# A fourth staging buffer, zeros moved to the K steps, and the weight-gradient stores of three groups moved to Pool's queue, in a decode-attention and FFN backward kernel

## The chip, the cores and the metric

One core of one Trainium2 chip. The metric is device time in microseconds (us), the median of several executions of the same program. A profiled execution gives a trace; its span, from the first to the last instruction, is some 1.8 us shorter than the time of that execution. The kernel before ran at 285.98 us (285.46 to 286.58, three executions). The core moves data with 16 DMA engines. Instructions on SP (SyncE), ACT (ScalarE) and Pool (GpSimd) put transfers into three queues, which the profile names q1, q10 and q0. Below, "the rings" are what waits in these queues, and a "hole" is a stretch in which they run dry and the rate falls.

## The reference

The kernel computes the output and all weight and input gradients of a layer that adds attention over a cache and a GEGLU FFN. Attention reads only the last 1024 of 4096 cache rows, but the gradients of the two caches are written whole, so three quarters of each are zeros.

```python
def _fwd_reference(A_x, A_k_cache, A_v_cache, A_wq, A_wo, B_x, B_w_gate, B_w_up, B_w_down):
    # attention: B=4, 32 heads of q, 8 of k and v, Dh=128, Sk=4096, window W=1024
    #   k, v = cache[:, :, Sk-W:, :];  o = softmax(q k^T / sqrt(Dh)) v;  o @ wo
    # ffn: (gelu(x @ w_gate) * (x @ w_up)) @ w_down      D=512, F=1792
    xn = _layernorm(x, axis=-1)
    return x + _A_ref(xn, ...) + _B_ref(xn, ...)

# outputs: (out, d x, d k_cache, d v_cache, d wq, d wo, d w_gate, d w_up, d w_down), bf16
# ... cut
```

The two cache gradients are 33.5 MB each. Of these, 64 rows of 786 KB (one for each batch and head of each cache) are zeros, 50.3 MB. That makes 81 MB written and 31 MB read.

## The kernel before

Heads are worked on in four groups, t = 0 to 3, of two K/V heads. For each group, scores run over V and K in eight steps each, softmax and its gradient follow, and each of dv and dk is evacuated from PSUM through staging buffers of 1 MB. `zeros(n)` queues n zero rows on ACT's queue. `bg` is a list of small pieces of work that `tick` puts between the matmuls.

```python
with tc.tile_pool(name="stage", bufs=3, reuse_waits="tile") as stage, ...:
    for t in range(NT):
        ...
        scores(t, 0, {})
        zeros(2 if t == 0 else 0)
        scores(t, 1, softmax(t))            # zeros(4) after each 2nd step of a head
        d1, d2 = softmax_d(t)
        zeros(4 if t >= NT - 2 else 0)
        ...
        odq(t); fin(t)
        load_next(t)                        # weights and K/V of group t + 2, Pool's queue
        tick(len(bg))
        dw(t)                               # pieces of dwo, dwq

# one dv or dk block of a head, 8 pieces
if jj == 0:
    held["stg"] = stage.tile([P, NQ, JQ, Dh], BF16, name="stg_" + nm, tag="stg")
... matmul into kv_ps, evac(stg[:, :, jj, :], mps[:], 512) ...
if jj == JQ - 1:
    store(nc.sync, out=og[:, t * GP + g, K0:Sk, :]..., in_=stg[:]..., ...)

# dw(t): four 0.52 MB stores a group, from the pool of four osb buffers
held["osb"] = outp.tile([P, rep, D], BF16, name="osb_o", tag="o")
...
store(nc.sync, out=out_5[...], in_=held["osb"][:], ...)

def zeros(n):
    zs = ztile[0:P:P // ZP, :]              # ZP = 64 partitions, 12 KB each
    ...
    z = store(nc.scalar, zdst, zsrc, "zeros", ["rest", "zeros"])
# ... cut
```

Of the kernel before, what the change touches and what calls it, by code (L numbers as in the profile page):

```python
# [13 lines left out]
BF16 = mybir.dt.bfloat16  # L14
P = 128
# [3 lines left out]
def kernel(  # L19
# [27 lines left out]
    nc = tc.nc  # L47

    B, Sq, D = A_x.shape
# [3 lines left out]
    rep = Hq // G  # L53
# [3 lines left out]
    ND = D // P  # L57
# [3 lines left out]
    GP = 2  # L61
    NT = G // GP
    HG = GP * rep
# [5 lines left out]
    CW = HG * Dh  # L69
# [177 lines left out]
                                  in_=tps[:].rearrange("p c (b r) -> p c b r", b=B)[:, :, :, 0:8])  # L247


    xnm = const.tile([P, rep, D], BF16, name="xnm")  # L250
    dym = ffn.tile([P, rep, D], BF16, name="dym")
    for src, dst in ((dy_b, dym), (xn_b, xnm)):
        for i in range(rep):
            nc.gpsimd.tensor_scalar(out=dst[:, i, :], in0=src[:], scalar1=msk_i[:, i:i + 1], scalar2=None,
                                    op0=ALU.mult)


# [124 lines left out]
    def masks(t):  # L382
        for k, nm in enumerate(("do", "q")):
# [3 lines left out]
                                        in1=msk[:, :, g].unsqueeze(2).broadcast_to([P, NQ, Dh]), op=ALU.mult)  # L387
            st[t][nm] = mr

    def scores(t, k, hooks):  # L390

        lf = (qm, dom)[k]
        blks = (k_t, v_t)[k]
        ps = ps_a.tile([P, WQ], FP32, name="S_ps", tag=("S", "dP")[k])
        for g in range(GP):
            for q in range(NQ):
                T_ps = ps_w.tile([P, JQ, P], BF16, name="T_ps", tag="w")
                for jj in range(JQ):
                    nc.tensor.transpose(T_ps[:, jj, :], blks[(t, g)][:, q * JQ + jj, :], ident[:])  # L399
                T_sb = tsb.tile([P, WQ, B], BF16, name="T_sb", tag="T", bufs=4)  # L400
                evac(T_sb[:].rearrange("p n b -> p (n b)"), T_ps[:].rearrange("p j m -> p (j m)"), 1024, half=True)
                s = q * GP + g
                for b in range(B):
                    nc.tensor.matmul(ps[b * RG:(b + 1) * RG, :], lhsT=lf[:, b, s * RG:(s + 1) * RG],  # L404
                                     rhs=T_sb[:, :, b], start=(g == 0 and q == 0),
                                     stop=(g == GP - 1 and q == NQ - 1), tile_position=(0, b * RG))
                for f in hooks.get(g * NQ + q, ()):
                    f()
                tick(2 if k or q % 2 else 1)
                if q == 1:  # L410
                    zeros(4 if (g, k) != (0, 0) else 0)
        st[t][("S", "dP")[k]] = ps[:]

    def by_batch(src, nm, eng):
# [133 lines left out]
    def dw(t):  # L548

        X = st[t]["X"]  # L550

        def piece_o(g, i, held):
            if i == 0:
                held["osb"] = outp.tile([P, rep, D], BF16, name="osb_o", tag="o")
            mps = ps_w.tile([P, D], FP32, name="dwo_ps", tag="w")
            nc.tensor.matmul(mps[:], lhsT=X[:].rearrange("p h d -> p (h d)")[:, g * rep + i:CW:HG], rhs=dyz[:], start=True, stop=True)  # L556
            evac(held["osb"][:, i, :], mps[:], 512)
            if i == rep - 1:
                store(nc.sync, out=out_5[t * CW:(t + 1) * CW, :].rearrange("(p k) n -> p k n", k=HG)[
                    :, g * rep:(g + 1) * rep, :], in_=held["osb"][:], kind="rest", apart=["zeros", "rest"])  # L560

        def piece_q(c2, k, held):
            if k == 0:
                held["osb"] = outp.tile([P, 2, GP, rep * Dh], BF16, name="osb_q", tag="o")
            ci, g = k // GP, k % GP
# [3 lines left out]
                             rhs=X[:, g * rep:(g + 1) * rep, :].rearrange("p i d -> p (i d)"), start=True, stop=True)  # L569
            evac(held["osb"][:, ci, g, :], mps[:], 512)  # L570
            if k == 2 * GP - 1:
                store(nc.sync,
                      out=out_4.rearrange("(p c) j -> p c j", c=ND)[:, c2 * 2:(c2 + 1) * 2, t * CW:(t + 1) * CW],
                      in_=held["osb"][:].rearrange("p c g j -> p c (g j)"), kind="rest", apart=["zeros", "rest"])

# [108 lines left out]

    acc_sum(0, [(lambda c, fc=fc: wd_sb[:, fc, c * P:(c + 1) * P], aT_b[:, fc, :]) for fc in range(NF)])

    def f_rows(srcT, nm):

        ps = od_ps[:]
        for f4 in range(NF4):  # L690
            for b in range(B):
                nc.tensor.matmul(ps[b * RB:b * RB + 4, f4, :], lhsT=srcT[:, 4 * f4:4 * f4 + 4, b], rhs=ident[:],
                                 start=True, stop=True, tile_position=(0, b * RB))
        rows = const.tile([P, NF4, P], BF16, name=nm)
        evac(rows[:], ps, 512)
        return rows

    a_r = f_rows(aT_b, "a_r")
    def piece_d(f4, i, n, held):
        if i == 0:  # L700
            held["osb"] = outp.tile([P, 4, D], BF16, name="osb_d", tag="o")
# [8 lines left out]
    def piece_g(s_r, og, c, i, held):  # L710
        if i == 0:
            held["osb"] = outp.tile([P, NF4, 4, P], BF16, name="osb_g", tag="o")
        n = (NF - i + 3) // 4
        mps = ps_w.tile([P, NF4, P], FP32, name="dwg_ps", tag="w")
        nc.tensor.matmul(mps[:, 0:n, :].rearrange("p f d -> p (f d)"), lhsT=xnm[:, i, c:D:ND],  # L715
                         rhs=s_r[:, 0:n, :].rearrange("p f d -> p (f d)"), start=True, stop=True)
        evac(held["osb"][:, 0:n, i, :], mps[:, 0:n, :], n * P)
        if i == 3:
# [9 lines left out]
    df_ps = ps_a.tile([P, ND, B], FP32, name="df_ps", tag="S")  # L728
    edge = dict(lhsT=ztile[0:1, 0:P], rhs=ztile[0:1, 0:ND * B])
    nc.tensor.matmul(df_ps[:].rearrange("p c b -> p (c b)"), start=True, stop=False, **edge)  # L730
    for srcT, wsb, og, nm in ((dhgT_b, wg_sb, out_6, "dhg_r"), (dhuT_b, wu_sb, out_7, "dhu_r")):
        s_r = f_rows(srcT, nm)
        for c in range(ND):
            held = {}
            for i in range(4):
# [17 lines left out]
    acc_add(1, df_ps[:])  # L753

    ffn_pools.close()
    with tc.tile_pool(name="stage", bufs=3, reuse_waits="tile") as stage, \
            tc.tile_pool(name="wodd", bufs=1, reuse_waits="tile") as wodd:
        wpool.append(wodd)
        kvpool.append(wodd)
# [3 lines left out]
        for t in range(NT):  # L763
# [4 lines left out]
            zeros(2 if t == 0 else 0)  # L768
            scores(t, 1, softmax(t))
            d1, d2 = softmax_d(t)  # L770
            zeros(4 if t >= NT - 2 else 0)
            if t + 1 < NT:
                pre(t + 1, {0: [d1], 2: [d2]})
            else:
# [78 lines left out]
```

## Time and profile before

| | before |
|---|---|
| time, median (range) | 285.98 us (285.46 to 286.58) |
| span of the profiled execution | 281.7 us (that execution took 283.50 us) |
| TensorE, VectorE, ScalarE, Pool busy | 75%, 56%, 41%, 20% |
| moved | 112.15 MB, mean 398 GB/s |
| plateau of the rate | 420 to 424 GB/s |

The page cuts the span into 40 slices. Its GB/s row says what the 16 DMA engines moved in each. The busy-by-stretch view gives the same for any stretch: length, busy time of PE (TensorE), PEld (weight loads), DVE, ACT and Pool, each with its number of instructions, then granted clock, DMA share and GB/s. The prediction shows the lines of both.

### The profile page before, as it was taken

To read this page: it belongs to the slowest core of one execution; us is meant where nothing else is said; L and a number is where in the kernel's file an instruction comes from. 1 tells how busy PE (TensorE), PEld (TensorE's weight loads), DVE (VectorE), ACT (ScalarE), POOL (GpSimd) and SP (SyncE) were. 2 spreads that over 40 slices of the span, in tenths; PEclk is the share of its full clock that TensorE was granted. 3 is DMA by queue.
4 is the path that set the end of the run, shared out by engine and by line. 5 is a ranking of instruction groups with operands and counts; after the bars stand their busy time and mean duration, and the time that the engine had idled before them with its cause. 6 is when DMAs were issued, how large, how long until landed. Compare 5 with 4: busy or idle time off the path is not lost.

```text
span 281.7 us, 7190 instructions
## 1 busy us (share of the span) xinstructions
PE 210.1 (75%) x3132; PEld 135.9 (48%) x3132; DVE 158.7 (56%) x336; ACT 115.6 (41%) x214; POOL 56.0 (20%) x56
## 2 busy tenths in 40 slices
PE   1968976968769699967793399786963996878950
PEld 0856854634536465534461265454641654526520
DVE  6945754626467457645672137547651465367691
ACT  1421743344535146535421335435502563571540
POOL 3890003400200633020024060110050201002000
PEclk9975999979988989999999559979995999799795
DMA  7999999999999999999999969999999779999995
GB/s 236 445 398 426 423 405 413 408 418 419 422 427 426 420 425 417 425 422 425 428 420 409 406 202 347 425 426 426 416 427 429 318 301 409 428 427 423 419 416 221
DMA packets 19407, 112.15 MB, mean 398 GB/s; under 512 B 1440, under 2 KB 5040, under 8 KB 10416
## 3 DMA queue, kind: packets, MB, share of 16 engines
q10 hardware_dynamic: 4384, 50.34, 42.4%
q1 hardware_dynamic: 12304, 44.58, 39.1%
q0 software_dynamic: 2688, 16.78, 15.1%
q8 instruction: 24, 0.39, 0.5%
q14 instruction: 7, 0.06, 0.0%
HBM read 30.68 MB, written 81.01 MB: 396 GB/s over the span
## 4 chain that ended last, share of the span: by engine, by line
PE 45%; DMA 27%; DVE 16%; ACT 4%; issue 3%; POOL 2%; ACTq 0%; DVEq 0%; SPq 0%
DMA out_dram<-stg_dv 18%; PE T_ps L399 10%; PE kv_ps L537 8%; PE S_ps L404 6%; DMA out_dram<-osb_d 6%; DVE T_sb L101 4%; DMA out_dram<-ztile 4%; PE dwo_ps L556 3%; PE acc_ps L213 3%; PE dwq_ps L568 2%; POOL P_x L417 2%; PE wqT_ps L595 2%; PE wgT_ps L742 2%; PE od_ps L509 1%; PE dwg_ps L715 1%
## 5 line engine op out<-in xcount | busy, mean ns | idle before, releaser
L101 DVE COPY T_sb<-T_ps 128x1024 bf16<-128x1024 bf16 x64 | 43.8, 691 | 41.2 <-PE T_ps L399 40.8
L99 ACT CAST stg_dk<-kv_ps 128x512 bf16<-128x512 f32 x40 | 22.2, 589 | 54.0 <-PE kv_ps L537 36.0
L99 ACT CAST stg_dv<-kv_ps 128x512 bf16<-128x512 f32 x57 | 30.4, 593 | 30.0 <-PE kv_ps L537 30.0
L537 PE MATMUL kv_ps<-qmr,dS_x 128*128 128x512 bf16 x64 | 22.9, 448 | 16.9 <-ACT stg_dk L99 15.3
L537 PE MATMUL kv_ps<-domr,P_x 128*128 128x512 bf16 x64 | 22.8, 427 | 5.4 <-POOL P_x L417 4.8
L101 DVE CAST stg_dk<-kv_ps 128x512 bf16<-128x512 f32 x24 | 16.1, 686 | 17.8 <-PE kv_ps L537 17.6
L399 PEld LDWEIGHTS <-kb 128*128 128x128 bf16 x256 | 18.6, 105 | 10.7 <-issue 7.8
L399 PE MATMUL T_ps<-ident,kb 128*128 128x128 bf16 x256 | 23.4, 231 | 0.0
L386 POOL TENSOR_TENSOR domr<-r,msk 128x512 bf16<-128x512 bf16 x8 | 8.2, 1040 | 71.2 <-DVE r L379 71.2
L99 ACT CAST osb_g<-dwg_ps 128x512 bf16<-128x512 f32 (+1 forms) x28 | 14.1, 540 | 18.4 <-PE dwg_ps L715 11.5
L399 PE MATMUL T_ps<-ident,vb 128*128 128x128 bf16 x256 | 21.3, 226 | 0.0
L399 PEld LDWEIGHTS <-vb 128*128 128x128 bf16 x256 | 16.6, 102 | 6.9 <-issue 5.0
L417 POOL TENSOR_TENSOR P_x<-P_b,bmsk 128x1024 bf16<-128x1024 bf16 x4 | 7.6, 1894 | 56.3 <-ACT P_b L465 56.3
L404 PE MATMUL S_ps<-T_sb,dom 128*32 128x256 bf16 x128 | 12.7, 387 | 8.0 <-DVE T_sb L101 7.5
L99 ACT CAST osb_o<-dwo_ps 128x512 bf16<-128x512 f32 x25 | 14.5, 587 | 9.3 <-PE dwo_ps L556 8.5
L99 ACT CAST osb_q<-dwq_ps 128x512 bf16<-128x512 f32 x25 | 14.3, 588 | 8.4 <-PE dwq_ps L568 7.8
L595 PEld LDWEIGHTS <-wq_sb 128*128 128x128 bf16 x128 | 9.0, 103 | 16.7 <-issue 15.1
L101 DVE COPY woT<-woT_ps 128x1024 bf16<-128x1024 bf16 x16 | 11.0, 689 | 8.8 <-PE woT_ps L338 8.8
L101 DVE COPY wqT<-wqT_ps 128x1024 bf16<-128x1024 bf16 x16 | 11.0, 689 | 5.6 <-PE wqT_ps L595 5.5
L101 DVE COPY wgT<-wgT_ps 128x1024 bf16<-128x1024 bf16 x14 | 9.7, 692 | 7.2 <-PE wgT_ps L742 7.2
L595 PE MATMUL wqT_ps<-ident,wq_sb 128*128 128x128 bf16 x128 | 11.1, 230 | 3.5 <-issue 3.1
L556 PE MATMUL dwo_ps<-dyz,od_x 128*128 128x512 bf16 x32 | 13.4, 453 | 0.2 <-ACT osb_o L99 0.2
(214 smaller groups left out, 392.1 us busy)
## 6 DMA issues: line engine op xcount, KB each, us to landing
out_dram<-ztile ACTq DMA_DIRECT2D x15, 3072.0 KB, 18.9
out_dram<-stg_dv SPq DMA_DIRECT2D x8, 1024.0 KB, 20.0
out_dram<-stg_dk SPq DMA_DIRECT2D x8, 1024.0 KB, 13.1
kb<-in_A_k_cache_dram POOLq DMA_DIRECT2D x5, 1024.0 KB, 18.3
vb<-in_A_v_cache_dram POOLq DMA_DIRECT2D x5, 1024.0 KB, 25.4
out_dram<-osb_o SPq DMA_DIRECT2D x8, 512.0 KB, 14.7
out_dram<-osb_q SPq DMA_DIRECT2D x8, 512.0 KB, 16.7
out_dram<-osb_g SPq DMA_DIRECT2D x8, 448.0 KB, 15.2
```

What stands on the lines that cost most here:

```text
L99: last.append(nc.scalar.copy(out=out, in_=in_))
L101: return nc.vector.tensor_copy(out=out, in_=in_)
L213: nc.tensor.matmul(ps[:, c, :], lhsT=lf(c), rhs=rhs, start=(k == 0), stop=(k == len(terms) - 1))
L386: nc.gpsimd.tensor_tensor(out=mr[:, g], in0=st[t]["r4"][:, k, :].unsqueeze(1).broadcast_to([P, NQ, Dh]), in1=msk[:, :, g].unsqueeze(2).bro ...
L399: nc.tensor.transpose(T_ps[:, jj, :], blks[(t, g)][:, q * JQ + jj, :], ident[:])
L404: nc.tensor.matmul(ps[b * RG:(b + 1) * RG, :], lhsT=lf[:, b, s * RG:(s + 1) * RG], rhs=T_sb[:, :, b], start=(g == 0 and q == 0), stop=(g = ...
L417: eng.tensor_tensor(out=dst[:].rearrange("p j (m b) -> p (j m) b", b=B), in0=src[:].unsqueeze(2).broadcast_to([P, WQ, B]), in1=bmsk[:].uns ...
L537: nc.tensor.matmul(mps[:].rearrange("p q d -> p (q d)"), lhsT=src[:, jj, :], rhs=mr[:, g].rearrange("p q d -> p (q d)"), start=True, stop= ...
L556: nc.tensor.matmul(mps[:], lhsT=X[:].rearrange("p h d -> p (h d)")[:, g * rep + i:CW:HG], rhs=dyz[:], start=True, stop=True)
L568: nc.tensor.matmul(mps[:], lhsT=xnz[:, c:D:ND], rhs=X[:, g * rep:(g + 1) * rep, :].rearrange("p i d -> p (i d)"), start=True, stop=True)
L595: nc.tensor.transpose(wT_ps[:, i, c, :], wq_sb[:, c, h * Dh:(h + 1) * Dh], ident[:])
L742: nc.tensor.transpose(wT_ps[:, i, c, :], wsb[:, c, fc * P:(fc + 1) * P], ident[:])
```

## The change

The intent: give the staging pool a fourth buffer (its memory comes from letting five small FFN tiles share slots with attention tiles), queue more zeros in the first K steps of groups 2 and 3 and fewer elsewhere, and send dwo and dwq of groups 0 to 2 through Pool's queue, behind the loads.

```diff
-    with tc.tile_pool(name="stage", bufs=3, reuse_waits="tile") as stage, \
+    with tc.tile_pool(name="stage", bufs=4, reuse_waits="tile") as stage, \

+    ZN = ((0, 4, 4, 4), (0, 4, 4, 2), (2, 4, 4, 4), (4, 4, 4, 4))
                 if q == 1:
-                    zeros(4 if (g, k) != (0, 0) else 0)
+                    zeros(ZN[t][GP * k + g])
-            zeros(4 if t >= NT - 2 else 0)
+            zeros(4 if t == NT - 1 else 0)

     def dw(t):
+        eng = nc.gpsimd if t + 1 < NT else nc.sync
-                store(nc.sync, out=out_5[...
+                store(eng, out=out_5[...
-                store(nc.sync, out=out_4...
+                store(eng, out=out_4...

-    xnm = const.tile([P, rep, D], BF16, name="xnm")
+    xnm2 = [attw.tile([P, rep // 2, D], BF16, name="xnm", tag=tag, bufs=1) for tag in ("od_x", "dST")]
-        rows = const.tile([P, NF4, P], BF16, name=nm)
+        rows = attw.tile([P, NF4, P], BF16, name=nm, tag=tag, bufs=1)   # tags E_f, Gt, dS_x
 # ... cut: the uses of these tiles
```

More of the change, by code (lines that the diff above doesn't have):

```diff
@@ L247 @@
                                   in_=tps[:].rearrange("p c (b r) -> p c b r", b=B)[:, :, :, 0:8])
-    xnm = const.tile([P, rep, D], BF16, name="xnm")
+    xnm2 = [attw.tile([P, rep // 2, D], BF16, name="xnm", tag=tag, bufs=1) for tag in ("od_x", "dST")]
     dym = ffn.tile([P, rep, D], BF16, name="dym")
-    for src, dst in ((dy_b, dym), (xn_b, xnm)):
+    for src, dst in ((dy_b, [dym[:, i, :] for i in range(rep)]), (xn_b, [xnm2[i // 2][:, i % 2, :] for i in range(rep)])):
         for i in range(rep):
-            nc.gpsimd.tensor_scalar(out=dst[:, i, :], in0=src[:], scalar1=msk_i[:, i:i + 1], scalar2=None,
+            nc.gpsimd.tensor_scalar(out=dst[i], in0=src[:], scalar1=msk_i[:, i:i + 1], scalar2=None,
                                     op0=ALU.mult)
@@ L558, in piece_o @@
             if i == rep - 1:
-                store(nc.sync, out=out_5[t * CW:(t + 1) * CW, :].rearrange("(p k) n -> p k n", k=HG)[
+                store(eng, out=out_5[t * CW:(t + 1) * CW, :].rearrange("(p k) n -> p k n", k=HG)[
                     :, g * rep:(g + 1) * rep, :], in_=held["osb"][:], kind="rest", apart=["zeros", "rest"])
@@ L571, in piece_q @@
             if k == 2 * GP - 1:
-                store(nc.sync,
+                store(eng,
                       out=out_4.rearrange("(p c) j -> p c j", c=ND)[:, c2 * 2:(c2 + 1) * 2, t * CW:(t + 1) * CW],
@@ L685, with f_rows @@
     acc_sum(0, [(lambda c, fc=fc: wd_sb[:, fc, c * P:(c + 1) * P], aT_b[:, fc, :]) for fc in range(NF)])
-    def f_rows(srcT, nm):
+    def f_rows(srcT, nm, tag):
         ps = od_ps[:]
@@ L693, in f_rows @@
                                  start=True, stop=True, tile_position=(0, b * RB))
-        rows = const.tile([P, NF4, P], BF16, name=nm)
+        rows = attw.tile([P, NF4, P], BF16, name=nm, tag=tag, bufs=1)
         evac(rows[:], ps, 512)
         return rows
-    a_r = f_rows(aT_b, "a_r")
+    a_r = f_rows(aT_b, "a_r", "E_f")
     def piece_d(f4, i, n, held):
@@ L714, in piece_g @@
         mps = ps_w.tile([P, NF4, P], FP32, name="dwg_ps", tag="w")
-        nc.tensor.matmul(mps[:, 0:n, :].rearrange("p f d -> p (f d)"), lhsT=xnm[:, i, c:D:ND],
+        nc.tensor.matmul(mps[:, 0:n, :].rearrange("p f d -> p (f d)"), lhsT=xnm2[i // 2][:, i % 2, c:D:ND],
                          rhs=s_r[:, 0:n, :].rearrange("p f d -> p (f d)"), start=True, stop=True)
@@ L730 @@
     nc.tensor.matmul(df_ps[:].rearrange("p c b -> p (c b)"), start=True, stop=False, **edge)
-    for srcT, wsb, og, nm in ((dhgT_b, wg_sb, out_6, "dhg_r"), (dhuT_b, wu_sb, out_7, "dhu_r")):
-        s_r = f_rows(srcT, nm)
+    for srcT, wsb, og, nm, tag in ((dhgT_b, wg_sb, out_6, "dhg_r", "Gt"), (dhuT_b, wu_sb, out_7, "dhu_r", "dS_x")):
+        s_r = f_rows(srcT, nm, tag)
         for c in range(ND):
```

## The prediction

> **What bounds the kernel now.** I read the page's first three parts, then the chain of work that ended last, the waits, the list of DMA issues in order of time, and busy time in chosen stretches. No engine is full over the span, but the DMA rows are:
>
> ```profile
> span 281.7 us, 7190 instructions
> PE 210.1 (75%) x3132; PEld 135.9 (48%) x3132; DVE 158.7 (56%) x336; ACT 115.6 (41%) x214; POOL 56.0 (20%) x56
> ...
> DMA  7999999999999999999999969999999779999995
> GB/s 236 445 398 426 423 405 413 408 418 419 422 427 426 420 425 417 425 422 425 428 420 409 406 202 347 425 426 426 416 427 429 318 301 409 428 427 423 419 416 221
> DMA packets 19407, 112.15 MB, mean 398 GB/s; under 512 B 1440, under 2 KB 5040, under 8 KB 10416
> ```
>
> A slice is 7.04 us. The DMA digit is 9 and the rate some 420 GB/s in nearly all slices, whatever the compute engines do: a plateau. It is left in four places: the start (236), slices 24 and 25 (202, 347), slices 32 and 33 (318, 301), and the end (221). The bytes cannot change (the outputs are written in full), so the plateau alone needs 112.15 MB / 421 GB/s = 266.4 us; the other 15.3 us of the span are the start, the end and the two holes. The busy-by-stretch view sizes the holes (its last two columns are DMA share and GB/s):
>
> ```profile
> 161.00:166.00 5.00, 4.71 (x85) 3.69 (x84) 1.77 (x6) 1.66 (x3) 2.34 (x4) 0.50 0.40 133
> ...
> 168.00:172.00 4.00, 4.00 (x43) 2.26 (x44) 2.15 (x4) 2.03 (x4) 0.10 (x1) 0.96 0.90 229
> 172.00:221.00 49.00, 35.89 (x554) 22.97 (x553) 25.35 (x50) 19.56 (x37) 5.78 (x4) 0.90 1.01 424
> 221.00:231.00 10.00, 10.00 (x122) 5.92 (x118) 6.65 (x11) 6.06 (x11) 2.04 (x2) 1.00 0.64 261
> 231.00:278.00 47.00, 33.62 (x417) 19.32 (x417) 29.76 (x58) 20.95 (x40) 3.79 (x2) 0.89 1.01 421
> ```
>
> Time lost against 421 GB/s: 5 x (421 - 133)/421 = 3.4 us; 4 x (421 - 229)/421 = 1.8 us; 10 x (421 - 261)/421 = 3.8 us. Together 9.0 us. That is the purse this change can win.
>
> Why the holes exist is in the chain that ended last (start, duration, what), here around the first hole:
>
> ```profile
> 130.20 1.08 ACT stg_dv L99 x2
> 131.30 27.25 DMA out_dram<-stg_dv
> ...
> 158.65 0.59 ACT stg_dk L99
> 159.28 0.59 PE kv_ps L537
> ...
> 162.34 1.86 PE acc_ps L213 x64
> ```
>
> A group t evacuates four 1 MB blocks into staging: dv of its two heads, then dk of its two. With three buffers the second dk block needs the buffer of the first dv block. That store is issued at 131.3 and is not done until 158.6, because 7.5 MB were already queued on the DMA rings. So ACT waits 9.5 us, TensorE behind it 8.6 us; in that time the rings drain, since whatever would feed them (the next four loads, which wait for the last reads of wo and wq at 163.7, the second dk store, the dw stores, the next zeros) comes later in program order. The same happens in the group after: store issued at 191.3, wait until 215.6.
>
> ```profile
> ACT stg_dk L99 <- DMA out_dram<-stg_dv: 17.8, 3, 9.5
> ...
> PE kv_ps L537 <- ACT stg_dk L99: 15.3, 2, 8.6
> ```
>
> (total us, times, longest.) 17.8 is 9.5 + 7.7 + about 0.6 in group 0.
>
> **What the Trainium skill says.** "DMA: Bandwidth & Descriptors", section "Issuing engines are not separate DMA queues": DMAs from sync, scalar and gpsimd run on the same 16 engines and interleave. The trace agrees: the rate is 424 in 172 to 221 us, where Pool's last four loads are still moving, and 421 in 231 to 278, where Pool's queue is empty. Moving stores to Pool therefore buys order, not bandwidth. The same page, "Where 436 GB/s comes from", puts the fabric ceiling at 435; the plateau here is 421 to 424, so there is little above it to win. "Trainium Kernel Development and Optimization", section "Best Practices", says that consistent bubbles can mean that SBUF or PSUM ran out; the two waits for a staging buffer are that case. "SBUF — State Buffer", section "SBUF: two separate sides", warns that a DMA from GpSimd can starve while VectorE runs a two-port mode. In this trace Pool's loads take 0.53 to 0.76 us to issue, also between copies by DVE, so I see no sign of it.
>
> **The change part by part.**
>
> Fourth staging buffer. The rotation becomes one buffer per block of a group, reused a whole group later, some 55 us, against landings of at most 24 us. All three waits go. TensorE's 8.6 us at 150 and 6.7 us at 209 leave the compute chain: everything after 159 moves 8.6 us earlier, everything after 216 moves 15.3 us. The last compute, now at 275.6, could end at about 260.3. DMA needs longer, so the end becomes the drain of the rings. The memory comes from xnm, a_r, dhg_r, dhu_r, which now share slots with attention tiles. Their readers, the dwg pieces, end by 77 us; the first attention writer, E_f, only replaces a_r, last read at 41; Gt, dS_x, dST and od_x are written after 77. No new wait with a cost. The second pool behind the staging shifts by one buffer; its loads wait until 41.76 us for the last read of the FFN weights already, and still will.
>
> Zeros in the first K steps. 64 rows of 786 KB in all, before and after: group 1 gives up 2 rows in its last V step, group 2 gives up the 4 after its softmax, group 2 gets 2 and group 3 gets 4 in the middle of the first head of K. They are fed exactly where the rings ran dry: 1.57 MB (3.7 us of work) and 3.15 MB (7.5 us).
>
> Does the supply then suffice? I add bytes issued less bytes moved at 0.42 MB per us, with the issue times of before shifted as above. Before, that backlog was 4.6 MB at 150.4 us and empty at 162, and empty again from 221 to 229. After: 3.1 MB at 150.4 (the two rows taken from group 1), 1.1 MB at 155.1, when the four loads come (+4.2 MB), 5.5 at 157 with the second dk store, 6.3 after the new zeros at about 159, 8 to 9 from 165 to 183, 6.7 at 191, 3.8 at 200, 1.7 at 207 after the last dk store of group 2, **0.9 at 210.5**, its lowest, then 3.4 with the new zeros of group 3, 7 to 10 from 220 to 240, some 3.5 left when compute ends. It never reaches zero: all three holes should close. The second (168 to 172) was the wq load in 2 KB packets alone on the rings; beside zeros and stores it should be hidden.
>
> dwo and dwq through Pool. 3 groups x 4 stores x 0.52 MB = 6.3 MB leave SP's queue for Pool's. Twelve issues of some 0.4 us at SP become some 0.6 us at Pool, 7 us of Pool over the run, in stretches where it idles (14 us ahead of each P_x). The dv stores of the next group no longer queue behind them; with four buffers nobody waits for that. A price: bytes over queue time (page part 3) give 16.78/(0.151 x 281.7) = 394 GB/s on Pool's queue against 405 on SP's, so 6.3 MB cost perhaps 0.4 us more.
>
> Sum: 9.0 won, less 0.4 for Pool's queue, less 0.6 for what stays of the holes (my allowance for the thin spot at 210 us) = 8.0 us. 285.98 - 8.0 = **278.0 us**, a span near 273.7.
>
> **The rivals.** (1) The gain is smaller because the holes are only filled in part: with 0.9 MB left on one queue at 210 us the 16 engines may already be uneven, as in 225 to 231 where lone small stores moved 268 GB/s. That could leave 2 to 3 us: 280 to 281. Against it: the backlog sum has margin everywhere else. (2) Pool becomes a wait: its queue is in order, so the four stores stand ahead of P_x, which releases the dv matmuls. The last of them was issued at 121.6 and P_x began at 123.5, so some 1 us of slack; a late descriptor would delay compute by 1 us a group. But compute now has some 9 us of slack against the drain (260 against 270), so this costs nothing unless Pool's ring fills and blocks it for longer: about 280. (3) Transfers were hidden anyway, the end is set by compute: then 15.3 us would be won, 271. The plateau forbids it: 266.4 us of DMA plus some 3 us of start and 3.7 us of end. (4) Zeros queued late delay the last stores, and the tail grows. Only order changes, not the sum of bytes, so I give it under 1 us.
>
> **Range and chances.** The full purse with the tail a little better gives about 275.5; half a purse lost gives 281.5. The 2% line is 280.26, so 5.7 of 9.0 us must come through. Faster by over 2%: 0.82; within 2%: 0.17; slower: 0.01.
>
> **What would show it.** Right: no wait of ACT's stg_dk on a DMA, TensorE without a gap of 7 to 9 us ahead of kv_ps, Pool's loads of group 3 issued near 155, the GB/s row at 400 or more from slice 2 to the last but one, the last compute 8 us or more ahead of the last landing, and a chain that ends in a long DMA. Wrong: a slice under 380 in the middle (rival 1), P_x later after P_b than today's 0.1 us, or gaps filled by waits for osb buffers (rival 2), or a plateau under 415 (Pool's stores slower than I allow).

## More of the kernel before

One more reading is used throughout: 421 GB/s over 16 engines is 26.3 GB/s for one (an estimate by division), so a rate of 25 to 29 GB/s means that one engine alone is moving, and 100 that about four are.

## The result

| | before | after |
|---|---|---|
| time, median of four executions | 286.12 us (285.46 to 286.58) | 281.65 us (281.13 to 281.97) |
| ratio | | 0.9844, 95% interval 0.9819 to 0.9869 |
| span of the profiled execution | 281.7 us | 279.4 us |

Ratios are the mean time of one kernel's executions over that of the other's in the same rounds, so they are not quite the ratio of the medians. The change is 4.5 us (1.6%) faster by the medians, where 8.0 us was predicted. It stays within 2%, and 281.65 lies just outside the range that ended at 281.5. The profiled execution of before (283.50 us) was quicker than each of the four timed ones, so the two traces are only 2.3 us of span apart. I use them for where time went, and the timed executions for how much.

The page of the changed kernel: span, busy time, then the DMA rows by slice.

```profile
span 279.4 us, 7192 instructions
PE 210.2 (75%) x3126; PEld 136.6 (49%) x3132; DVE 158.4 (57%) x336; ACT 115.1 (41%) x214; POOL 63.7 (23%) x68
...
DMA  7999999999999999999999999999999999999970
GB/s 237 447 388 430 425 406 402 414 421 427 420 419 427 425 419 419 418 429 432 421 421 364 394 392 429 428 423 421 425 423 427 408 424 424 420 427 424 421 316 20
DMA packets 18655, 112.15 MB, mean 401 GB/s; under 512 B 1456, under 2 KB 5056, under 8 KB 9664
```

Both holes are gone: slices that stood at 202 and 318 GB/s are at 392 and above, and one mild dip (364) is left. What is new is the end. The last slice shows 20 GB/s over 7 us, where before it showed 221. Busy time by stretch of the changed kernel says when, and what the other engines did (columns as explained above):

```profile
149.00:161.00 12.00, 10.36 (x155) 7.27 (x154) 7.14 (x13) 7.03 (x13) 7.75 (x11) 1.00 1.00 370
161.00:172.00 11.00, 8.55 (x86) 5.02 (x85) 5.96 (x13) 4.61 (x11) 1.68 (x3) 1.00 1.00 411
...
221.00:231.00 10.00, 7.31 (x71) 4.09 (x70) 5.23 (x12) 4.67 (x10) 2.06 (x4) 1.00 1.00 417
231.00:270.00 39.00, 27.71 (x356) 16.15 (x355) 25.20 (x47) 17.49 (x32) 3.46 (x2) 0.88 1.01 421
...
270.00:272.00 2.00, 0.00 (x0) 0.00 (x0) 0.00 (x0) 0.00 (x0) 0.00 (x0) 0.50 0.39 154
272.00:274.00 2.00, 0.00 (x0) 0.00 (x0) 0.00 (x0) 0.00 (x0) 0.00 (x0) 0.50 0.07 30
274.00:276.00 2.00, 0.00 (x0) 0.00 (x0) 0.00 (x0) 0.00 (x0) 0.00 (x0) 0.50 0.08 29
276.00:278.00 2.00, 0.00 (x0) 0.00 (x0) 0.00 (x0) 0.00 (x0) 0.00 (x0) 0.50 0.06 23
```

The rate is 421 until 270 us and compute is over by 268. From 272 to 278 us it is 23 to 30 GB/s: one engine is still moving, and fifteen have nothing left. The same view of the kernel before, around its first hole and at its end:

```profile
161.00:172.00 11.00, 10.71 (x141) 7.07 (x140) 5.28 (x11) 4.60 (x8) 4.44 (x6) 0.67 0.71 221
...
163.00:164.00 1.00, 1.00 (x44) 1.00 (x42) 0.17 (x1) 0.00 (x0) 0.34 (x1) 0.50 0.09 33
...
276.00:278.00 2.00, 0.00 (x0) 0.00 (x0) 0.00 (x0) 0.00 (x0) 0.00 (x0) 0.50 1.04 409
278.00:280.00 2.00, 0.00 (x0) 0.00 (x0) 0.00 (x0) 0.00 (x0) 0.00 (x0) 0.50 0.28 105
```

Before, the tail is some 2 us with about four engines. But inside the hole there is a microsecond at 33 GB/s (and, read in the same way, one at 29 GB/s at 228 us in the last hole): there, too, a lone engine was still working while the others waited for work. I took the hole for idle time of all sixteen.

An account in time lost against 421 GB/s, from these two views (each term is the length of the stretch times the missing share of 421):

| stretch, us | lost before | lost after | difference |
|---|---|---|---|
| 149 to 161 | 12 x (421 - 414)/421 = 0.2 | 12 x (421 - 370)/421 = 1.5 | +1.3 |
| 161 to 172 | 11 x (421 - 221)/421 = 5.2 | 0.3 | -4.9 |
| 221 to 231 | 3.8 (prediction) | 0.1 | -3.7 |
| 270 to the end | 3.4 | 8.3 | +4.9 |
| sum | | | -2.4 |

(The end: what is left of the span after 270, less the bytes moved there over 421. After, 9.4 us less 0.47 MB; before, 11.7 us less 3.5 MB.) The sum agrees with the 2.3 us between the two spans. The holes gave back nearly what I said, but the end took 4.9 us.

The waits of the changed kernel (total us, times, longest) show that the wait on staging is gone and a smaller one, on the four osb buffers, has appeared:

```profile
ACT osb_o L99 <- DMA out_dram<-osb_o: 6.5, 2, 5.2
...
PE dwo_ps L560 <- ACT osb_o L99: 4.9, 1, 4.9
...
ACT osb_q L99 <- DMA out_dram<-osb_q: 4.2, 2, 3.2
```

Its cause is the chain's longest piece, a store that Pool issued behind 4 MB of loads in its queue. The first line is from the chain of the changed kernel (start, duration, what), the second from its view of the tile osb_o:

```profile
160.82 48.97 DMA out_dram<-osb_o
```

```profile
DMA to landing us min/median/max: 13.8/26.0/49.0
```

Before, the longest landing of an osb_o store was 14.7 us. The last instruction of compute ended at 268.0 us, where I had predicted 260.3. The rate nevertheless stayed at 421 GB/s from 231 to 270, so compute did not set the end. The dip at 149 to 161 (370 GB/s) is not a hole of the old kind: the engines' share is 1.00 there, so they were busy and moved less.

### The profile page after: what moved, and what is told of

Read it like the earlier page. It is cut to its first block, busy times and chain, and to the rows that moved or that the text cites. A ratio compares the mean times of both kernels' runs of the same rounds, so it can differ in the third digit from the quotient of the medians.

```text
span 279.4 us, 7192 instructions
## 1 busy us (share of the span) xinstructions
PE 210.2 (75%) x3126; PEld 136.6 (49%) x3132; DVE 158.4 (57%) x336; ACT 115.1 (41%) x214; POOL 63.7 (23%) x68
## 4 chain that ended last, share of the span: by engine, by line
PE 45%; DMA 27%; DVE 17%; issue 3%; ACT 2%; POOL 1%; another core or an unknown queue 0%; ACTq 0%; DVEq 0%; SPq 0%
DMA out_dram<-osb_o 18%; PE T_ps L402 9%; PE kv_ps L540 8%; DMA out_dram<-osb_d 6%; PE S_ps L407 5%; DVE T_sb L101 5%; DMA out_dram<-ztile 4%; PE dwo_ps L560 3%; PE acc_ps L213 2%; PE od_ps L512 2%; PE wqT_ps L599 2%; PE woT_ps L339 2%; PE wgT_ps L746 2%; POOL P_x L420 1%; PE dwg_ps L719 1%
## 5 line engine op out<-in xcount | busy, mean ns | idle before, releaser
L402 PEld LDWEIGHTS <-kb 128*128 128x128 bf16 x256 | 18.3, 105 | 10.6 <-issue 7.9
L540 PE MATMUL kv_ps<-qmr,dS_x 128*128 128x512 bf16 x60 | 19.7, 412 | 1.8 <-DVE dS_x L420 1.4
L407 PE MATMUL S_ps<-T_sb,dom 128*32 128x256 bf16 x128 | 12.7, 386 | 8.3 <-DVE T_sb L101 7.8
L560 PE MATMUL dwo_ps<-dyz,od_x 128*128 128x512 bf16 x32 | 14.1, 481 | 4.9 <-ACT osb_o L99 4.9
L407 PE MATMUL S_ps<-T_sb,qm 128*32 128x256 bf16 x128 | 13.1, 389 | 3.7 <-DVE T_sb L101 3.7
L407 PEld LDWEIGHTS <-dom 128*32 128x32 bf16 x128 | 5.3, 93 | 17.2 <-issue 15.3
L339 PE MATMUL woT_ps<-ident,wo_sb 128*128 128x128 bf16 x128 | 11.4, 237 | 2.7 <-DVE stg_dv L101 1.9
## 6 DMA issues: line engine op xcount, KB each, us to landing
out_dram<-osb_g SPq DMA_DIRECT2D x8, 448.0 KB, 15.3
```

The costliest lines, as they stand in the source:

```text
L339: nc.tensor.transpose(wT_ps[:, i, c, :], wo_sb[:, 2 * h2 + i, c * P:(c + 1) * P], ident[:])
L402: nc.tensor.transpose(T_ps[:, jj, :], blks[(t, g)][:, q * JQ + jj, :], ident[:])
L407: nc.tensor.matmul(ps[b * RG:(b + 1) * RG, :], lhsT=lf[:, b, s * RG:(s + 1) * RG], rhs=T_sb[:, :, b], start=(g == 0 and q == 0), stop=(g = ...
L540: nc.tensor.matmul(mps[:].rearrange("p q d -> p (q d)"), lhsT=src[:, jj, :], rhs=mr[:, g].rearrange("p q d -> p (q d)"), start=True, stop= ...
L560: nc.tensor.matmul(mps[:], lhsT=X[:].rearrange("p h d -> p (h d)")[:, g * rep + i:CW:HG], rhs=dyz[:], start=True, stop=True)
```

## The experiments

All theories agree on what closes the holes. They differ on what holds the end near 278 us. **Theory A**: the stores on Pool's queue (their 49 us, the osb waits). **Theory B**: one of the 16 engines is behind all along and never idle any more, so the end is its own work and not the drain of the rings. Later the question became why it is behind. "Before" was run again and gave medians of 284.59, 284.36, 284.12, 284.16 and 284.29 us; ratios are to those. The changed kernel itself was not repeated, so runs are compared with it through the ratios (its own is 0.9844). Spans and rates are from each run's profile.

### The parts of the change, one by one

**e1: the change without Pool's stores.**

```diff
-        eng = nc.gpsimd if t + 1 < NT else nc.sync
+        eng = nc.sync
```

> The changed kernel with one part undone: all dwo and dwq stores go out through SP again; four staging buffers and the new zeros stay. Theory A (Pool's queue is the culprit: the stores wait there behind 4 MB of loads, hold the osb buffers, and one DMA engine ends 7 us after the rest because of it): no wait of ACT's osb_o on a DMA, the tail at under 150 GB/s shrinks from 8 us to 2 us or less, about 277 us. Theory B (one DMA engine falls behind in the loads of group 3 whoever stores dw, and the holes of the kernel before only hid it): the tail stays at 5 us or more, 280 to 282 us, though the osb waits go.

Measured: 281.69 us, ratio 0.9881 (0.9833 to 0.9929), span 280.2. No osb_o store held anybody up for long, and yet there is the same end: 364 GB/s in 270 to 272, then 124, 37 and 25. Theory A falls: without its suspect the end is the same, and the time too within the intervals (0.9881 against 0.9844).

**e2: the fourth buffer alone** (zeros and dw stores as in before).

```diff
-    with tc.tile_pool(name="stage", bufs=3, ...
+    with tc.tile_pool(name="stage", bufs=4, ...      # and the shared tiles that pay for it
```

> The kernel before plus the fourth staging buffer alone (dw through SP, zeros where they were). By the backlog sum of the prediction the rings are nearly dry at 159 to 165 and at 207 to 214 without the new zeros: part of the holes stays, 279 to 282 us by theory A. By theory B the tail of one engine is there too unless a hole lets it catch up: 281 to 283 us.

Measured: 281.72 us, 0.9889 (0.9842 to 0.9936), span 279.8. **e3: the dw stores on Pool alone** (three buffers, zeros as in before; the shared tiles stay).

```diff
-                store(nc.sync, ...
+                store(nc.gpsimd if t + 1 < NT else nc.sync, ...
```

> The kernel before with dwo and dwq of the first three groups through Pool alone: three staging buffers, zeros where they were. Theory A: the staging waits stay, the stores of group 1 and 2 land 20 us later or more, the holes get no smaller, 286 to 288 us and a longer tail than the 2 us of before. Theory B: as before, 285 to 287 us, tail 2 us.

Measured: 281.41 us, 0.9873 (0.9826 to 0.992), span 279.1. Both theories had expected hardly any gain here (285 to 288), so both missed. Moving the dw stores out of SP's queue lets the stg_dv store land early enough that no wait of stg_dk on a DMA is left among the waits listed, even with three buffers. In e2, four buffers with the old zeros let compute run ahead into other waits: ACT's stg_dv waits 12.9 us for osb_o stores and 7.3 for a stg_dk store. Both runs still have a hole. Busy by stretch, first e2, then e3:

```profile
262.00:266.00 4.00, 3.90 (x21) 1.63 (x18) 3.33 (x6) 2.59 (x5) 0.00 (x0) 0.65 0.13 49
...
272.00:274.00 2.00, 0.00 (x0) 0.00 (x0) 1.90 (x3) 0.00 (x0) 0.00 (x0) 1.00 0.84 326
274.00:276.00 2.00, 0.00 (x0) 0.00 (x0) 0.00 (x0) 0.00 (x0) 0.00 (x0) 0.77 0.07 28
276.00:278.00 2.00, 0.00 (x0) 0.00 (x0) 0.00 (x0) 0.00 (x0) 0.00 (x0) 0.50 0.07 26
```

```profile
223.00:225.00 2.00, 2.00 (x17) 0.80 (x15) 0.69 (x1) 0.81 (x2) 0.38 (x1) 0.50 0.06 23
...
274.00:276.00 2.00, 0.00 (x0) 0.00 (x0) 0.00 (x0) 0.00 (x0) 0.00 (x0) 0.50 0.31 114
276.00:278.00 2.00, 0.00 (x0) 0.00 (x0) 0.00 (x0) 0.00 (x0) 0.00 (x0) 0.50 0.06 22
```

In e2 the others run dry for 4 us at 262 and one engine goes on (the 49 is a mean that falls to 25); all sixteen share the work again, and one is still the last. In e3 it is alone at 223 to 225. Closing such a hole does nothing for the engine that never stopped in it. e3 shows it best: its hole of 221 to 231 us (263 GB/s) is as large as in the kernel before (261), and yet it is as fast as e5 below, which has closed it (425) and has no dip of this depth elsewhere: 0.9873 and 0.9875. This fits three quite different kernels ending within 0.3 us of each other.

**e5: e1 with the last four loads of group 3 moved from Pool's to SP's queue.**

```diff
-        eng = nc.gpsimd if t else nc.sync
+        eng = nc.gpsimd if t not in (0, NT - 1) else nc.sync
-        (nc.gpsimd if GP * t + g > GP else nc.sync).dma_start(...
+        (nc.gpsimd if GP * t + g > GP and (t, g) != (NT - 1, 1) else nc.sync).dma_start(...
```

> As e1, and the last four loads of group 3 (wo, wq, K and V of its second head), which move slowly in both kernels, go out through SP instead of Pool. If it is Pool's descriptors that make them slow (packets of 8 KB up to 1.3 us against 0.31), the dip in GB/s after 149 us goes and the time falls 1 to 2 us below e1. If it is the data's place in memory or the mix with the stores, the dip stays and the time is that of e1 within 0.5%.

Measured: 281.37 us, 0.9875 (0.9813 to 0.9936), span 279.8. The dip at 149 to 161 us, for which this run was made, is smaller (397 GB/s against 322 in e1), and the time is that of e1. Most engines are done by 270, earlier than in any other run so far, and the lone engine moves 25 and 26 GB/s from 272 to 278. The others end at about 270, 271, 272, 274 or 275 (e5, the change, e1, e2, e3): the last byte comes between 277.7 and 278.7 in all of them. Of theory B, this stands: the end is set by one engine's own work.

### Changing what the engines carry

**e6 and e7: two zero rows (1.57 MB) written from 8 partitions**, in e6 partitions 0 to 56, in e7 64 to 120.

```diff
+            if og is out_2 and r == 30:      # these two rows only; all else as in e1
+                zn = ztile[0:57:8, :]         # e7: ztile[64:121:8, :]; 8 times 12 KB of each
+                parts = [... one transfer a row ...]
```

> e1 (fourth buffer, new zeros, dw through SP) with one pair of zero rows, 1.57 MB of 112, written from 8 partitions of the lower half instead of 64, so that only eight of the 16 DMA engines carry it: these get 98 KB more, 3.7 us at 26.5 GB/s each, the other eight 98 KB less. Theory B (the end is set by one slow engine): if the slow one is among the relieved eight, the last landing moves 3.7 us earlier, the time 2 to 3.7 us below e1, 278 to 279.7; if it is among the loaded eight, 3.7 us later, about 285. Theory A, or an end set by compute: within 0.5 us of e1.

> As e6 with the 8 partitions of the upper half. If the partition chooses the engine, the other eight are loaded and the sign is opposite to that of e6 (278 to 279.7 against 285, by theory B). If the order within the transfer chooses it, the same as e6.

Measured: 288.02 us (1.0122, 1.0072 to 1.0172) and 296.98 us (1.0421, 1.0359 to 1.0483). In e6 the rate at the end is 83 GB/s for 4 us and then 39, so several engines end late. In e7 the rate is 280 GB/s from 167 to 192 us and the last engine stops at 295. My sizes were off. What follows is only that loading some engines unevenly moves the end by many microseconds with every byte and all the work of compute unchanged, and that which partitions feed it matters as well (9 us between the two).

**e11 and e12: the same rows from the lower or the upper 64 partitions.**

```diff
+                zn = ztile[0:64, :]           # e12: ztile[64:128, :]
```

> e1 with the same pair of zero rows (1.57 MB) read from the 64 partitions of the lower half instead of every second partition. If the partition chooses the engine, eight engines carry 196 KB each (3.7 us more) and eight are relieved by 3.7 us. e6 and e7 differed by 9 us, so the slow engine should be one of the upper half: here it is relieved, its end moves from 277.7 to 274, the others' from 272 to 275.7: about 2 us below e1, 279.6. If the end is not set by one slow engine, no gain.

> The mirror of e11: 64 partitions of the upper half. By theory B the slow engine gets 3.7 us more: about 285.4, and a longer tail of a single engine.

Measured: 281.90 us (0.9899, 0.9832 to 0.9966) and 282.35 us (0.9918, 0.9836 to 0.9999), both with the lone engine at 25 and 28 GB/s in 276 to 278. The expectation that halves of the partitions belong to halves of the engines missed: these transfers ran on all 16 engines wherever their partitions lie. (The trace's DMA records hold one packet of four bytes for each engine that a transfer used, see below; here they are 16 a row, in e6 and e7 eight.)

**e13 and e14: one of the two rows from the lower 64 partitions, the other from 24** (64 to 87 in e13, 72 to 95 in e14).

```diff
-                for k, (p0, m) in enumerate(((0, 64), (0, 64))):      # e11
+                for k, (p0, m) in enumerate(((0, 64), (64, 24))):     # e14: (72, 24)
```

> One row of the pair from the lower half, one from partitions 64 to 87: [...]the two engines[...] carry nothing of this pair (3.7 us less), the other upper six 1.2 us more, the lower eight as before. If the slow engine is one of these two: end near 274, 278. If it is one of the other upper six: end 1.2 us later, 282.8.

> Control of e13: partitions 72 to 95, so that the two engines[...] are spared. If the slow engine is one of these two: 278; otherwise 282.8. At most one of e13 and e14 can gain.

Measured: 283.81 us (0.9963, 0.9887 to 1.0038) and 285.81 us (1.0044, 0.9961 to 1.0126). In e13 there is no lone engine: 139 GB/s on average from 272 to 278, and all over soon after. In e14 a lone one ends at 282 (26 GB/s). The mapping from partitions to engines that their expectations rest on is shown by no run here. By the same count of packets, the row from 24 partitions ran on 12 engines in both, so these were not the tests that I meant. They are inconclusive on which engine it is, but neither is faster.

### Why one engine is behind

In the trace's DMA records a transfer ends with packets of four bytes, one for each engine that carried it: 16 for nearly all transfers here. The Trainium skill says why ("DMA: Bandwidth & Descriptors", section "Why a DMA increments its semaphore by 16 and not by 1"): each engine writes its own +1 when its share has landed. The time from the median to the last of the 16 is therefore how far the slowest engine is behind. I worked it out from those records; it is not a view of the profile. For the zeros of the changed kernel it is 1.1 to 1.3 us until 90 us, goes up and down between 1.2 and 3.2 until 195, and then, from 208 us on, is 3.2, 4.2, 4.6, 7.5, 10.6 and 10.1 us. The last zero was complete on fifteen engines at 265.4 us and on the last at 272.9.

The same measure shows what a hole did in the kernel before. Zeros complete at 220 us had their last engine 2.4 us behind the median; those complete at 239, after the hole of 221 to 231, 0.1 us; those at 259 again 2.9. In the changed kernel, without the hole, it is 4.2 us at 222 and 7.5 at 241.

So I took the program apart. None of the next four computes the result; all write the right number of bytes to every output.

**e10: the 81 MB of stores alone**, half on SP's and half on ACT's queue, no compute, no loads. **e16: e10 with 3072 matmuls beside it. e17: e10 with 280 DVE and 180 ACT copies. e18: the stores on ACT's queue, with 28 K/V loads of 1 MB on SP's.**

```diff
 # e10: 16 stores of 4 cache rows + the weight gradients, from a tile of zeros
 # e16
+    for i in range(24):
+        mps = ps.tile([P, 4, P], FP32, name="mps", tag="m")
+        for k in range(128):
+            nc.tensor.matmul(mps[:, k % 4, :], lhsT=w[:], rhs=z[:, 0:P], start=True, stop=True)
+        nc.vector.tensor_copy(out=o[:], in_=mps[:])
 # e17
+    for i in range(280):
+        nc.vector.tensor_copy(out=a[:], in_=z[:, 0:1024])
+    for i in range(180):
+        nc.scalar.copy(out=b[:], in_=z[:, 0:1024])
 # e18
+    for i in range(28):
+        nc.sync.dma_start(out=t_[:]..., in_=src[:, (i // 2) % 8, K0:4096, :]...)
```

> No compute: all outputs written with zeros through SP and ACT, 80 MB, wrong results on purpose. If one DMA engine is slower by itself (8 us in 277, 3%), it ends some 5 us after the others here too: several us at 26 GB/s at the end. If only the work beside it (loads, instruction fetches, the engines' traffic) slows it, all 16 end within 1 us.

> The stores of e10 beside 3072 matmuls, wrong results on purpose. If TensorE's instruction stream makes one engine late (fetches, or whatever goes with instructions), the last landing is 3 us or more after the median engine's; else within 1 us, as in e10, but for two fetches of 0.93 us.

> The stores of e10 beside 280 copies on VectorE and 180 on ScalarE, wrong results on purpose. If SBUF traffic or instructions of these engines make one DMA engine late: 3 us or more between the median and the last; else within 1 us.

> The stores of e10 through ACT beside 28 loads of 1 MB (K and V of the window) through SP, wrong results on purpose. If reading makes one engine late: the last lands 2 us or more after the median; else within 1 us.

Measured, in this order: 202.16, 211.92, 345.84 (its copies run on long after the stores; span 344.1) and 265.13 us. The GB/s rows of e10 and of e16 in 40 slices (5.0 and 5.3 us each):

```profile
span 200.4 us, 71 instructions
...
GB/s 0 314 419 419 419 417 420 419 419 419 419 419 419 419 419 424 414 419 419 427 410 419 419 427 420 422 422 424 422 419 419 420 422 442 419 419 444 433 418 276
```

```profile
span 210.1 us, 6240 instructions
PE 175.1 (83%) x3072; PEld 173.5 (83%) x3072; DVE 20.1 (10%) x26; POOL 0.2 (0%) x4
...
GB/s 0 332 419 412 415 418 416 418 404 421 418 418 413 418 419 419 416 418 418 421 418 416 421 416 413 416 426 421 418 418 421 430 424 429 418 432 418 398 87 19
```

The stores are the same. Alone, the sixteen engines stop together, from 418 to nothing. With matmuls the mean rate over most of the span is only a few GB/s lower, but the last two slices are at 87 and 19. By stretch, e16:

```profile
200.00:202.00 2.00, 0.00 (x0) 0.00 (x0) 0.00 (x0) 0.00 (x0) 0.50 0.35 151
202.00:204.00 2.00, 0.00 (x0) 0.00 (x0) 0.00 (x0) 0.00 (x0) 0.50 0.05 22
204.00:206.00 2.00, 0.00 (x0) 0.00 (x0) 0.00 (x0) 0.00 (x0) 0.50 0.07 29
206.00:208.00 2.00, 0.00 (x0) 0.00 (x0) 0.00 (x0) 0.00 (x0) 0.50 0.07 29
```

A tail like that of the changed kernel, without its attention, its loads, its Pool queue or its buffers. In e17 the stores end as in e10 while DVE copies up to 134 us and ACT from 150 on; in e18 the end is sharp too:

```profile
194.00:196.00 2.00, 0.00 (x0) 1.94 (x3) 0.00 (x0) 1.00 1.00 423
196.00:198.00 2.00, 0.00 (x0) 1.97 (x2) 0.00 (x0) 1.00 1.08 459
198.00:200.00 2.00, 0.00 (x0) 1.94 (x3) 0.00 (x0) 1.00 0.32 133
200.00:202.00 2.00, 0.00 (x0) 1.94 (x3) 0.00 (x0) 1.00 0.00 0
```

```profile
GB/s 256 348 426 431 426 431 424 432 424 432 424 432 424 432 424 429 427 429 427 429 427 427 431 427 429 427 429 429 427 429 427 429 427 429 433 436 438 423 425 309
```

So neither these copies nor a mixture of loads and stores makes an engine late by more than 0.8 us (median to last). What goes with TensorE's instructions does. One thing that goes with them is fetching them. e16 has 6240 instructions, e17 533, and the page lists fetches as a queue of their own (packets, MB, share). First e16, then e19, the run with half the matmuls below; e10, e17 and e18 have no such line:

```profile
q8 instruction: 24, 0.39, 0.7%
```

```profile
q8 instruction: 12, 0.20, 0.3%
```

The records tie the delays to these fetches. After the first 12 us, 66 of the 8800 large packets (8 KB or more) of e16 took over 1.3 times their usual time, and all 66 start within 2 us before or 1.2 us after one of the 24 fetches. In e19 it is 34, all around its 12 fetches; in e10 and e18 none, in e17 six. So in time the slow packets go with the fetching of the instructions, not with the matmuls at large. How that makes one engine later than the others is not shown.

**e15: e1 with every load moved from Pool's to SP's queue**, so that Pool starts no DMA at all.

```diff
-        eng = nc.gpsimd if t else nc.sync
+        eng = nc.sync
-        (nc.gpsimd if GP * t + g > GP else nc.sync).dma_start(...
+        nc.sync.dma_start(...
```

> e1 with all loads through SP as well, so that Pool issues no DMA at all. If Pool's descriptors make one engine late, the lone tail goes and the time falls to 276 to 278. If not, the end stays at 277 to 278 us of the span with a lone engine, 281 to 282 us (plus what loads waiting in SP's queue cost).

Measured: 284.62 us, 1.0009 (0.9953 to 1.0065), span 282.1. The loads now stand in the way of stores in one queue (332 GB/s from 162 to 168), so all is later, but the lone engine is still there:

```profile
276.00:278.00 2.00, 0.00 (x0) 0.00 (x0) 0.00 (x0) 0.00 (x0) 0.00 (x0) 0.50 0.08 33
278.00:280.00 2.00, 0.00 (x0) 0.00 (x0) 0.00 (x0) 0.00 (x0) 0.00 (x0) 0.50 0.07 26
```

Pool's queue is therefore not what makes it late, and e16 has none either.

**e19: e16 with half the matmuls.**

```diff
-    for i in range(24):
+    for i in range(12):
```

> Wrong results on purpose: the stores alone, with 12 x 128 matmuls beside them instead of 24 x 128. Dose: with 3072 matmuls one DMA engine was 8.0 us late at the end and the span was 210.1 us (202 to 208 with a lone engine); without any, 200.4. If the lateness goes with TensorE's instructions, it grows to about 4 us until some 90 us and then stays: last-minus-median of a transfer's completions 3.5 to 4.5 us at the end, span about 204.5 to 206, a lone engine for about 4 us. If it were a matter of the chip or of any TensorE work at all, 8 us again (210); if a threshold, 200.4.

Measured: 204.93 us, span 203.1. The page has TensorE busy for 88.2 us, up to slice 19 of 40, and by stretch the last matmul ends at some 95 us. How far the slowest engine is behind at the end of each transfer of SP's queue (median to last of the 16 completions; again from the records):

| end of the transfer at, us | 26 | 46 | 66 | 87 | 107 | 127 | 147 | 166 | 175 |
|---|---|---|---|---|---|---|---|---|---|
| e10, no matmuls | 0.1 | 0.1 | 0.1 | 0.2 | 0.1 | 0.1 | 0.1 | 0.2 | 0.2 |
| e19, matmuls to 95 us | 1.7 | 2.1 | 2.9 | 3.7 | 3.7 | 3.5 | 3.2 | 2.9 | 2.8 |
| e16, matmuls to 183 us | 1.9 | 2.1 | 2.8 | 3.6 | 4.9 | 5.8 | 6.8 | 7.4 | 8.0 |

The two lie on one line while both run matmuls. When e19's stop, its lateness stops growing at 3.7 us and slowly shrinks. It grows with the matmuls run, 3.7 us for 1536 and 8.0 for 3072 (of which 1.7 to 1.9 is there by 26 us), and as well with the fetches, 12 and 24: these two runs don't tell the two apart. Nor does this dose carry over to the changed kernel: there 2395 matmuls had run by 194 us with 2.1 us of lateness (of the zeros), and 8.5 us more came with the next 614. I had expected 3.5 to 4.5 at the end and a span of 204.5 to 206; the shrinking made it a little less.

### Trying to win the time back

**e20: the change, with four zero rows mostly from 60 partitions. e21: two zero rows mostly from 35.** The same section of the Trainium skill says that a transfer of SP's or ACT's queue uses the largest number of engines, up to 16, that divides the slowest dimension of both sides, and the lowest-numbered ones. By that, 60 partitions spare engine 15, and 35 (7 engines) spare 7 to 15. The records agree on the counts, 15 and 7 packets of four bytes for these transfers; they do not tell which engines.

```diff
+            if og is out_3 and r == 8:                               # e20: 4 rows, e21: 2 rows
+                for m, a, b in ((60, 0, 2880), (64, 2880, K0)):      # e21: (35, 0, 3045), (27, 3045, K0)
+                    zn = ztile[0:m, :]                               # writes cache rows a to b
```

> The changed kernel, with four zero rows written from 60 partitions (2880 of their 3072 cache rows; the other 192 from 64 partitions). By the Trainium skill's rule the 60-partition transfer uses 15 engines, the lowest-numbered, so engine 15 carries 184 KB less (7.1 us at 26 GB/s) and the others 12 KB more (0.5 us). If the late engine is number 15: the lone tail goes, 277 to 278.5 us. If it is another: 281.5 to 282.5, a lone tail as in the changed kernel. If the rule doesn't hold and 16 engines carry it: the same as the changed kernel.

> The changed kernel, with two zero rows written from 35 partitions: by the same rule 7 engines (0 to 6) carry them, so each of those gets 126 KB more (4.8 us at 26 GB/s) and each of 7 to 15 gets 98 KB less (3.8 us). If the late engine is among 7 to 15: it ends near 274 us of the span and engines 0 to 6 near 275.5 to 276: no lone engine at the end but some seven, 279.5 to 280.5 us. If it is among 0 to 6: it ends near 283, alone: 286 us or more. With the run of 60 partitions this tells: 15, one of 7 to 14, or one of 0 to 6.

Measured: 287.01 us (1.0098, 1.0046 to 1.0151) and 287.70 us (1.0118, 1.0056 to 1.018): both slower. By stretch, e20 and then e21:

```profile
200.00:210.00 10.00, 6.93 (x117) 5.09 (x115) 5.49 (x11) 3.40 (x7) 3.33 (x3) 1.00 0.98 314
274.00:280.00 6.00, 0.00 (x0) 0.00 (x0) 0.00 (x0) 0.00 (x0) 0.00 (x0) 0.50 0.44 181
```

```profile
213.00:218.00 5.00, 3.71 (x40) 2.01 (x38) 3.03 (x5) 0.00 (x0) 0.00 (x0) 1.00 0.46 184
```

In e21 the rows came just where the backlog is thinnest: 184/26.3 = 7.0 engines worked for 5 us and nine stood idle. That agrees with the page's count of seven, and it made a new hole. In e20 the 12 KB packets took 625 ns on average in 200 to 210 us, where those of the changed kernel took 464, and some seven engines (181/26.3 = 6.9) ended late instead of one. Which engine is the late one, and whether giving it less would win the 5 us, stays open. No version here is faster than the changed kernel beyond the intervals, and e2, e3 (one part of the change alone) and e1 (one part left out) have most or all of its gain.

## Why the prediction was wrong

- **The bound and the holes: right.** The rate is the bound, and the holes were where and as large as said: 8.6 us of the 9.0 came back in those two places.
- **Their cause: right, but not the only cure.** With the fourth buffer no wait of stg_dk on a DMA is left. e3 shows that moving the dw stores out of SP's queue removes that wait as well.
- **What stays of the holes and of Pool's queue, 1.0 us: a little low.** 0.4 us of the holes stays, and the dip at 149 to 161 costs 1.3 us more than before. The 0.4 us for Pool's queue itself can't be told from the runs (e1, without it, is equal within the intervals).
- **Compute's end: wrong, without effect.** Predicted at 260.3, measured at 268.0. The osb wait, which the prediction had named as a sign of its second rival, came, but it explains little of this: in e1, without the store behind it, compute ended at 266.7. So the sum that moved all of compute up by the whole 15.3 us of waits was wrong; what held it instead was not worked out. The rings did not run dry.
- **"DMA needs longer, so the end becomes the drain of the rings": the step that failed.** I divided all bytes by the rate of all sixteen and took the end to be "3.7 us". Most engines did drain at 270 to 271 us, just as the sum says, and by 272 a single one was left. It ended at 278. The term of the end was mis-sized: the loss after 270 us was 3.4 before and 8.3 after, and the difference of 4.9 us, taken from the 7.3 that the middle won, leaves what the traces show.
- **Rival 4 ("under 1 us") came nearest, with the wrong reason.** The tail grew, but not for late zeros: e2, whose zeros are those of before, has the same end. Rival 2's waits came and cost nothing; rival 3 did not happen. Of rival 1 the sign came, a slice under 380 in the middle (364), but not where or why it was said: the thin spot at 210 us stayed at 420 or so, and in the dip the engines were busy.

**The cause.** Shown by the runs: one engine moves alone at the end in the change and in e1, e2, e3, e5, e11, e12 and e15; the end stays the same when the others finish 5 us earlier; matmuls with their fetches beside the same stores produce such a tail (e16), and half of them half the lateness (e19); copies (e17) and loads (e18) do not, and Pool's queue is not needed for it (e15). By the records, the engines were level after the last hole of the kernel before (0.1 us) and grew apart again where no hole followed.

Argued only: that it is always the same engine, and that the tail of the changed kernel has the cause of the tail in e16. The 33 and 29 GB/s in the holes of before, its tail of some 2 us and the holes of e2 and e3 fit this; the faster growth after 194 us does not by itself. Open: by what way TensorE's instructions slow one engine. The page lists 24 fetches of instructions (0.39 MB) in the kernel before, in the change and in e16. When I strung the packets of e2 into sixteen chains by their start and end times, the late chain carried none of those fetches; its ordinary packets took 12.7 us longer in all than their usual durations, those of the other chains up to 2.4. That is an inference from the records, not a view, and such chains can be swapped where packets of two engines end together; in e16, slow packets and fetches lie together in time (above). Whether recording the profile has a part in it is open too, as I have no look at single engines without it.

## What to carry to other kernels

This kernel, bound by DMA, ended with its slowest DMA engine, and a mean rate over sixteen hides that one: read the tail and the holes in stretches of 1 or 2 us, and divide by the rate of one engine. A rate of about a sixteenth inside a hole can mean that the hole is partly a catch-up, so that closing it gains less than its area, as here (8.6 us closed, 2.3 us of span gained). Before predicting what closing it is worth, compare the last of a transfer's completions with their median, long before the end.

## What the Trainium skill lacked or had wrong

- "DMA: Bandwidth & Descriptors", section "Latency and other measured facts", says that two of the engines are usually slower, with contention from Pool's descriptor rings as an uncertain best guess. Here an engine was 6.0 us (e15) and 8.0 us (e16) late with no DMA of Pool at all, and its lateness grew with TensorE's instructions and their fetches: 8.0 us for 3072 matmuls and 24 fetches, 3.7 for 1536 and 12, 0.2 for none. These runs do not tell the engine's number.
- No page works out what one late engine means for the end of a DMA-bound kernel: six microseconds at 23 to 30 GB/s after 421. None that I found says that packets are slow around fetches of instructions (all 66 slow packets of e16).
- The same page, section "Why a DMA increments its semaphore by 16 and not by 1", has the count of engines right for 35 partitions (184 GB/s, seven engines). It does not say that a transfer of 60 partitions may slow itself and the others: in 200 to 210 us of e20, 12 KB packets took 625 ns instead of 464, and 8 KB packets of SP's queue, which are not its own, some 400 instead of 310.
- The same page's "Issuing engines are not separate DMA queues" holds for bandwidth (421 GB/s from 231 to 270 us, as before), but a reader should know that a store can land very late in Pool's queue: one of 0.52 MB behind 4 MB of loads there took 49.0 us, against at most 14.7 for the same stores through SP. It cost no time that these runs show.
